# Expert 1's first weight matrix in 1 MB loads, one load of its second matrix at an earlier place, and VectorE's work beside the late tile in another order

## The chip, the cores and the metric

The kernel runs on one core of a Trainium2 chip. The metric is the device time of one execution in microseconds (us); times shown are medians of several executions on one chip. Beside these times there is one execution taken by the hardware profiler, from which every row below comes.

## The reference

Attention with decay gives a token matrix x of 3072 rows (4 batches of 768) by 512 (8 heads of 64). Each row then goes through one of 16 experts, which two small products choose.

```python
for t in range(S):                                   # S = 768, per batch and head
    state = gamma * state + outer(k[t], v[t])        # 64 x 64
    y[t] = scale * q[t] @ state
x = y.transpose(0, 2, 1, 3).reshape(3072, 512)
g = argmax(x @ w_group)                              # 4 groups
e = argmax(x @ w_expert[g])                          # 4 experts in a group
weight = softmax(group logits)[g] * softmax(expert logits)[e]
out[row] = weight * (relu(x[row] @ w1[g, e]) @ w2[g, e])   # 512 -> 1024 -> 512
```

## The kernel before, in words

**Two parts.** Attention runs in 12 steps of 128 tokens of two batches at once; what a step gives is written to `xd`, the matrix x in DRAM (the writes are those of line L356, on SyncE's queue). The router works on blocks of 4 chunks of 128 tokens while attention still runs: for every token it finds the expert, its rank in that expert's list (the rank matmuls L436 and L438), and adds the token to the lists by matmuls with one-hot matrices (`tally`, L522).

**Expert tiles.** An expert's tokens are gathered from `xd` by an indirect DMA on GpSimd (L775), transposed on TensorE (`tpx`, L793), split into a bf16 high part `xbh` (ScalarE, L795) and a low part `xbl` (VectorE, L818), and multiplied with the weights. The weights are loaded in f32 (`wf`, four buffers of 1 MB: two halves of w1, two of w2) and split likewise into `wh` (ScalarE, L751) and `wl` (VectorE, L753), eight pieces for one expert. Each product is three matmuls: high by high, high by low, low by high. The first layer goes to `hps` (L841, four quarters `f2`), and its relu is split into `hh` (ScalarE, L845) and `hl` (VectorE, L848).

**Order of the tiles.** Expert 0 comes in two: `ua`, its first 128 tokens, starts before attention has ended, and `ub`, the late tile (108 wide), takes the rest. Then follows `va` (expert 1, 236 wide), and then the other 14 experts, sorted on the chip by their number of tokens. The sort is `order()` on VectorE: `cnt`, `key`, two memsets, `gt` (L607), `pos` (L612), `eq` (L615), `eqk` (L620), `ordf` (L623), `ord` (L626). `own_counts()` then gives `ocols` (L583, L585), the width of `va`'s two parts, and `counts()` gives `cols` (L639 to L645), the widths of the sorted experts.

**How a width reaches TensorE.** `shape()` loads a width from memory into a register of TensorE's own sequencer (L806) and sets a shape from it (MOVE_SHAPE, L807). TensorE's sequencer works in program order, so matmuls behind such a load wait with it. The two loads of `ocols` stand behind the second and third part of `ub`'s second layer (L947), and the two loads of `cols` for the next expert in `va`'s first layer.

**What sets the order.** Nothing here is scheduled by a tool: the order on every engine is the order of the calls. `self.layers(u)` is a generator that stops between parts of a tile's matmuls, and the loops around it put other work at a stop numbered `i`. `first(n)` lets `ua`'s matmuls run n stops on; a stop in the first layer is 12 matmuls. `route_steps(n)` runs n steps of the router or of the sort. `beside(i, place)` puts loads and splits at places of attention step i.

Of the kernel before, what the change touches and what calls it, by code (L numbers as in the profile page):

```python
# [99 lines left out]


KX = (4, 6)
NEXT = {(10, 0): (0, 4), (10, 2): (4, 8)}
KEYED = (9, 10)


class Kernel:
# [1098 lines left out]
    def run(self):  # L1206
        tc, nc = self.tc, self.nc
        with ExitStack() as ctx:
# [18 lines left out]
            us = [dict(at=((j + 1) % 2, 0), W=(PW[-1:] + WIDTH)[j], pool=wpool[(j + 1) % 2]) for j in range(NS + 1)]  # L1227
            va = us[0]
# [4 lines left out]
            def pick(j):  # L1233
                self.picked(us[j], j - 1)

            def cols(j, i):
                return self.cols[0:1, i, j - 1:j] if j else self.own[:, i:i + 1]

            def first(n):

                for _ in range(n):
                    next(self.first, None)

            def early(i, k, high):
                if 0 <= i - 3 < 8:
                    self.wsplit(ua, 2 * i - 6 + k, 16, nc.gpsimd, high=high, low=not high)
# [9 lines left out]
            def beside(i, place):  # L1256

                last = i == NS2 - 1
                for k in range(*NEXT.get((i, place), (0,))):
                    self.wload_part(va, k)  # L1260
                if place == 5 and i == 10:
                    ua["mt"] = self.pairs()
                    self.tokens(ua["mt"][:, 0, 0:1], ua["mt"][:, 0, 1:2], self.lists[:, 0:1])
                    self.gather(ua)
                    self.known()
                if place == 0:
                    if 2 <= i <= 9:
                        for k in range(2):
                            self.wload_part(ua, 2 * i - 4 + k)
                if place == 4 and last:  # L1270
                    self.shape(ua, 4, 0, self.early_cols)
                if place == 0 and last:
                    early(i - 1, 0, False)
                    early(i - 1, 1, False)
                if place == 2 and last:
                    self.wsplit(va, 0, low=False)
                if place == 1:
                    if not last:
                        early(i - 1, 0, False)
                if place == 3 and last:  # L1280
                    self.xtrans(ua, "big", (0,))
                    self.wload(va, 2, nc.scalar)

            self.wp = pool("wp", 2)
            with ExitStack() as actx:
                apool = lambda name, bufs: actx.enter_context(tc.tile_pool(name=name, bufs=bufs))
                self.lp, self.vp = apool("lp", 1), apool("vp", 1)
                self.attention(extra, beside)
# [19 lines left out]
            late.append(self.late_entries(5, self.oh[:, 0:BM, 0:1]))  # L1308
            self.route_steps(99, True)
            assert not self.steps  # L1310
            first(3)
            self.wsplit(va, 2, low=False)
            next(route)
            while next(route) != "late":
# [8 lines left out]
                nc.vector.scalar_tensor_tensor(*h)  # L1323
            for _ in route:
                pass
            first(2)
            p, y = self.at
            ent = self.entries(5, *self.chosen(y, self.yp))
            self.spreads.append((self.marks(p, self.yp), ent))
# [2 lines left out]
            nc.gpsimd.memset(self.xg[1], 0.0)  # L1332
            self.wsplit(va, 3, low=False)
            self.steps.append(self.order())
            self.route_steps(5)
            for i, k in enumerate(self.first):
                if i == 0:
                    self.wsplit(va, 4, low=False)
# [5 lines left out]
                if i == 3:  # L1344
# [3 lines left out]
                    self.nc.vector.tensor_copy(ub["mt"][:, 0, 1:2], self.final[:, 0, 1, 1:2])  # L1348
                    va["mt"] = self.final[:, 1]
                    self.gather(va)  # L1350
            self.route_steps(99)
            assert not self.steps
            pick(1)
            pick(2)
            for u in us[1:3]:
                self.listed(u)
            self.own_counts()
            self.wsplit(va, 0, high=False)
            ub["wh"], ub["wl"] = ua["wh"], ua["wl"]
            self.gather(us[1])  # L1360
            for i, k in enumerate(self.layers(ub)):
                if i in (1, 3):
                    self.wsplit(va, 6 + i // 2, low=False)
                if i in (8, 12):
                    self.xtrans(va, ("sta", "big")[i // 4 - 2], (i // 4 - 2,))
                if i in (3, 7, 12, 13, 14):
                    low = (3, 7, 12, 13, 14).index(i) + 1
                    self.wsplit(va, low, high=False)
                    if low % 2:
                        self.wload(us[1], low // 2)  # L1370
                if i in (9, 10):
                    self.shape(va, 0, i - 9, cols(0, i - 9))
                if i == 15:
                    self.counts()
# [83 lines left out]
```

## Time and profile before

| | us |
|---|---|
| median of 3 runs | 406.8 (406.68 to 407.85) |
| the profiled execution | 405.67 |
| its span, first to last instruction | 403.9 |
| TensorE busy | 389.8 (97% of the span) |
| VectorE busy | 295.3 (73%) |
| ScalarE busy | 223.0 (55%) |
| GpSimd busy | 166.8 (41%) |

The profiled execution lasts 1.77 us longer than its span, and lies 1.13 us under the median of the runs. A busy share is a mean over the whole span; the stage that the change touches lies between 88 and 135 us, around the end of attention (about 104 us), and is read by itself. PE is TensorE's matmuls and PEld its weight loads, DVE is VectorE, ACT ScalarE, POOL GpSimd, SP SyncE; a q behind a name is the engine's sequencer.

### The profile page before, as it was taken

The page shows a single profiled execution, that of the slowest core. Times are in us where ns is not written, and L with a number is a line of the kernel's source. Part 1 is how long each engine was busy: PE and PEld are TensorE (multiplying, and loading weights), DVE is VectorE, ACT ScalarE, POOL GpSimd, SP SyncE. Part 2 cuts the span into 40 slices and gives each one's busy share as a digit, 9 for nine tenths or more (in the row PEclk, how much of TensorE's full clock was granted, in tenths as well). Part 3 has the DMA queues.
Part 4 walks back from the last instruction along what each step waited for, and adds up shares of the span by engine and source line. Part 5 has one row for each costly group of instructions (what it writes and reads, how often), then busy time and mean ns, then how long its engine had stood idle before and what let it go on. Part 6 is the DMA issues. An engine that isn't in the chain of part 4 may idle for free.

```text
span 403.9 us, 13857 instructions
## 1 busy us (share of the span) xinstructions
PE 389.8 (97%) x5809; PEld 324.4 (80%) x5841; DVE 295.3 (73%) x483; ACT 223.0 (55%) x340; POOL 166.8 (41%) x172
## 2 busy tenths in 40 slices
PE   9999999999998999999999999999999999999992
PEld 5789888888858878586978888797887978879792
DVE  4575876868798879886758686776878769788620
ACT  3224434544652765565566666676666767667520
POOL 4542769659585106131416234260522505232001
PEclk9999999999999999999999999999999999999997
DMA  7999999988816897887868787979789897887001
GB/s 254 356 346 346 317 355 292 355 283 290 288 69 208 304 363 263 264 262 246 252 228 267 258 298 262 299 276 320 260 282 330 274 325 268 256 333 278 11 32 36
DMA packets 38643, 107.13 MB, mean 265 GB/s; under 512 B 12020, under 2 KB 12148, under 8 KB 31156
## 3 DMA queue, kind: packets, MB, share of 16 engines
q1 hardware_dynamic: 28752, 92.52, 67.0%
q0 software_dynamic: 9536, 12.63, 8.9%
q10 hardware_dynamic: 292, 1.08, 0.8%
q8 instruction: 47, 0.77, 0.7%
q14 instruction: 16, 0.13, 0.1%
HBM read 94.18 MB, written 13.20 MB: 266 GB/s over the span
## 4 chain that ended last, share of the span: by engine, by line
PE 46%; issue 36%; POOL 10%; DVE 4%; ACT 1%; DMA 1%; POOLq 0%; SPq 0%; ACTq 0%; DVEq 0%
PE hps L841 12%; POOL out L999 6%; PE op L299 5%; PE yps L875 5%; PE sh L235 5%; POOL xg L775 4%; PE op L286 3%; PE yps L922 3%; PE sh L345 2%; PE stp L261 2%; PE yps L925 2%; PE sh L319 1%; PE sh L220 1%; PE log L332 1%; PE tpx L793 1%
## 5 line engine op out<-in xcount | busy, mean ns | idle before, releaser
L753 DVE TENSOR_TENSOR wl<-wf,wh 128x1024 bf16<-128x1024 f32 x120 | 145.1, 1220 | 36.9 <-ACT wh L751 33.0
L751 ACT ACTIVATE wh<-wf 128x1024 f16<-128x1024 f32 (+1 forms) x136 | 133.6, 1001 | 0.1
L841 PE MATMUL hps<-xbl,wh 128*128 128x128 f16 (+16 forms) x544 | 128.4, 249 | 0.7 <-issue 0.5
L841 PE MATMUL hps<-xbh,wh 128*128 128x0 bf16 x544 | 125.9, 241 | 0.3 <-issue 0.3
L841 PE MATMUL hps<-xbh,wl 128*128 128x0 bf16 x544 | 125.9, 241 | 0.2 <-issue 0.2
L999 POOL DMA_INDIRECT out<-yo,mt x30 | 39.1, 1303 | 159.0 <-ACT yo L981 121.1
L841 PEld LDWEIGHTS <-wh 128*128 128x128 f16 x1088 | 94.9, 98 | 1.5 <-issue 0.9
L925 PEld LDWEIGHTS <-wh 128*128 128x128 f16 x768 | 47.1, 97 | 22.9
L845 ACT ACTIVATE hh<-hps 128x256 bf16<-128x256 f32 (+16 forms) x68 | 34.1, 503 | 43.6 <-PE hps L841 41.6
L775 POOL DMA_INDIRECT xg<-xd,mt x30 | 51.8, 1727 | 13.1 <-issue 5.2
L841 PEld LDWEIGHTS <-wl 128*128 128x128 bf16 x544 | 53.1, 98 | 1.6 <-issue 0.9
L247 DVE TENSOR_TENSOR pf<-sh,tri 128x512 f32<-128x512 f32 x48 | 30.6, 685 | 22.7 <-PE op L299 8.3
L795 ACT ACTIVATE xbh<-tpx 128x512 bf16<-128x512 f32 (+14 forms) x32 | 16.7, 523 | 45.9 <-PE tpx L793 45.9
L848 DVE SCALAR_TENSOR_TENSOR hl<-hps,hh 128x216 f16<-128x216 f32 (+15 forms) x64 | 36.6, 574 | 4.2 <-ACT hh L845 3.7
L922 PE MATMUL yps<-wh,hh 128*128 128x512 f16 x96 | 36.4, 379 | 0.0
L922 PE MATMUL yps<-wh,hl 128*128 128x512 f16 x96 | 36.4, 379 | 0.0
L922 PE MATMUL yps<-wl,hh 128*128 128x512 bf16 x96 | 36.3, 378 | 0.0
L818 DVE TENSOR_TENSOR xbl<-tpx,xbh 128x512 f16<-128x512 f32 (+14 forms) x32 | 19.1, 597 | 20.0 <-ACT xbh L795 20.0
L925 PEld LDWEIGHTS <-wl 128*128 128x128 bf16 x384 | 24.2, 97 | 11.4
L192 POOL TENSOR_TENSOR vs<-lv,cst 128x512 f32<-128x512 f32 x24 | 24.6, 1043 | 14.9 <-DMA lv<-qkv 9.9
L925 PE MATMUL yps<-hl,wh 128*128 128x108 f16 (+11 forms) x384 | 29.1, 198 | 0.0
L925 PE MATMUL yps<-hh,wh 128*128 128x0 bf16 x384 | 26.6, 190 | 0.0
(194 smaller groups left out, 599.1 us busy)
## 6 DMA issues: line engine op xcount, KB each, us to landing
wf<-w2p SPq DMA_DIRECT2D x29, 1024.0 KB
wf<-w1p SPq DMA_DIRECT2D x28, 1024.0 KB
lq<-qkv SPq DMA_DIRECT2D x24, 256.0 KB
lk<-qkv SPq DMA_DIRECT2D x24, 256.0 KB
lv<-qkv SPq DMA_DIRECT2D x24, 256.0 KB
xd<-xr SPq DMA_DIRECT2D x22, 256.0 KB
wf<-w1p SPq DMA_DIRECT2D x16, 256.0 KB
wf<-w2p SPq DMA_DIRECT2D x8, 256.0 KB
```

Of the source, the lines that this page charges most:

```text
L192: self.nc.gpsimd.tensor_tensor(o, v, g, ALU.mult)
L235: nc.tensor.matmul(self.sh[2 * u + par][64 * half:64 * half + 64, cs], kT[rs, ks:ks + 64], qT[rs, cs], start=True, stop=True, skip_group_c ...
L247: nc.vector.tensor_tensor(o, sc, tri, ALU.mult)
L751: nc.scalar.activation(u["wh"][i][:, cs], u["wf"][i][:, cs], AF.Copy)
L753: (eng or nc.vector).tensor_tensor(u["wl"][i][:, cs], u["wf"][i][:, cs], u["wh"][i][:, cs], ALU.subtract)
L775: nc.gpsimd.indirect_dma_start(out=xg[0:r, i, :], out_offset=None, in_=self.xd[0:n, :], in_offset=bass.IndirectOffsetOnAxis(ap=mt[0:r, i, ...
L841: nc.tensor.matmul(o, l[:, k, fs], m, start=(n == 0), stop=(n == 11), skip_group_check=True)
L845: nc.scalar.activation(hh[:, f, 0:W], hv[:, :, 0:W], AF.Relu)
L848: nc.vector.scalar_tensor_tensor(*rest)
L922: nc.tensor.matmul(big, h[:, k, 0:P], w[k], start=(n == 0), stop=(n == 23))
L925: nc.tensor.matmul(o, w[k][:, d * P:d * P + P], m, start=(n == 0 and d == 0), stop=(n == 23), skip_group_check=True,)
L999: s = nc.gpsimd.indirect_dma_start(out=self.out, out_offset=bass.IndirectOffsetOnAxis(ap=mt[0:r, i, 0:1].bitcast(U32), axis=0), in_=yo[0:r ...
```

## The change

- Expert 1's w1 is loaded by two DMAs of 1 MB (L725) where eight of 256 KB (L739) stood, at the same places of step 10, on SyncE's queue.
- The first half of its w2, which ScalarE's queue issues, moves from place 3 to place 2 of the last step.
- `ua`'s first layer runs four stops ahead of the last rank matmuls where three stood (48 matmuls for 36), and one stop less later, so that seven of its eight stops lie ahead of the late tile's ids (L563) where six did.
- `order()` is cut at other places: `gt` and `pos` come behind the late tile's `xbl` and the final lists, and `eq` to `ocols` come inside `ub`'s first layer. One `wl` piece that stood ahead of `ub`'s `hl` is put between them, and the others move back by one place.
- The gather of the third tile stands behind a later stop in the code; on GpSimd itself the order of instructions stays as it was.

```diff
-NEXT = {(10, 0): (0, 4), (10, 2): (4, 8)}
+NEXT = {(10, 0): 0, (10, 2): 1}
...
-                for k in range(*NEXT.get((i, place), (0,))):
-                    self.wload_part(va, k)
+                if (i, place) in NEXT:
+                    self.wload(va, NEXT[i, place])
...
                 if place == 2 and last:
                     self.wsplit(va, 0, low=False)
+                    self.wload(va, 2, nc.scalar)
...
                 if place == 3 and last:
                     self.xtrans(ua, "big", (0,))
-                    self.wload(va, 2, nc.scalar)
...
-            first(3)
+            first(4)
             self.wsplit(va, 2, low=False)
...
-            first(2)
+            first(1)
...
             self.steps.append(self.order())
-            self.route_steps(5)
+            self.route_steps(3)
...
-            self.route_steps(99)
-            assert not self.steps
-            pick(1)
-            pick(2)
-            for u in us[1:3]:
-                self.listed(u)
-            self.own_counts()
-            self.wsplit(va, 0, high=False)
+            self.route_steps(2)
             ub["wh"], ub["wl"] = ua["wh"], ua["wl"]
-            self.gather(us[1])
             for i, k in enumerate(self.layers(ub)):
...
-                if i in (3, 7, 12, 13, 14):
-                    low = (3, 7, 12, 13, 14).index(i) + 1
+                if i == 1:
+                    self.wsplit(va, 0, high=False)
+                if i == 3:
+                    self.route_steps(2)
+                if i == 7:
+                    self.route_steps(99)
+                    assert not self.steps
+                    pick(1)
+                    pick(2)
+                    for u in us[1:3]:
+                        self.listed(u)
+                    self.own_counts()
+                if i == 10:
+                    self.gather(us[1])
+                if i in (7, 12, 13, 14, 15):
+                    low = (7, 12, 13, 14, 15).index(i) + 1
                     self.wsplit(va, low, high=False)
```

On VectorE, just ahead of the late tile's `xbl`, the sort's first steps stand so (a minus marks a row of before alone, a plus one of after; `key` is the sort key):

```order
 L603 MEMSET key 128x1
 L604 MEMSET key 128x1
-L607 TENSOR_TENSOR gt<-key 128x256
-L612 TENSOR_REDUCE pos<-gt 128x16
 L818 TENSOR_TENSOR xbl<-tpx,xbh 128x4x108
 L529 TENSOR_TENSOR lists<-lists,tally 128x160
```

`gt` and `pos` no longer stand ahead of `xbl`. They come back on VectorE behind the last of the list's instructions (L535, L1348):

```order
 L535 TENSOR_REDUCE final<-lists 128x32
 L1348 COPY mt<-final 128x1
+L607 TENSOR_TENSOR gt<-key 128x256
+L612 TENSOR_REDUCE pos<-gt 128x16
+L848 SCALAR_TENSOR_TENSOR hl<-hps,hh 128x2x108
+L753 TENSOR_TENSOR wl<-wf,wh 128x1024
+L848 SCALAR_TENSOR_TENSOR hl<-hps,hh 128x2x108
 L615 TENSOR_TENSOR eq<-pos,rest 128x256
 L620 TENSOR_TENSOR eqk<-eq,rest 128x256
+L848 SCALAR_TENSOR_TENSOR hl<-hps,hh 128x2x108 x2
 L623 TENSOR_REDUCE ordf<-eqk 128x16
 L626 CAST ord<-ordf 128x16
```

Between L1348's copy and `ordf`, and so ahead of `ocols`, stand seven more instructions than before: `gt`, `pos`, four `hl` of the late tile and one `wl` piece of expert 1. On ScalarE, in the last attention step, the load of w2 stands so:

```order
 L391 ACTIVATE ex<-log 128x80
 L751 ACTIVATE wh<-wf 128x1024
+L725 DMA wf<-w2p 128x2048
 L324 ACTIVATE ls<-sh_117 128x256
 L353 ACTIVATE pf<-sh_118 128x512
 L353 ACTIVATE pf<-sh_119 128x512
 L795 ACTIVATE xbh<-tpx 128x4x128
-L725 DMA wf<-w2p 128x2048
 L324 ACTIVATE ls<-lgt 128x256
```

The load moved ahead of four instructions, among them the transposed output's copies `pf`, which the next writes to `xd` read.

## Rows read from the trace of the kernel before

**Rows 1.** Length, then busy us of PE, PEld, DVE, ACT, POOL; clock, DMA share, GB/s.

```profile
135.00:398.00 263.00, 261.31 (x3257) 214.86 (x3281) 198.08 (x234) 164.45 (x228) 82.80 (x54) 1.00 0.75 256
```

**Rows 2.** Timeline of PE: start, duration, line, tile, and the idle time before.

```profile
106.49 0.22 PE L841 MATMUL hps<-xbh,wl 128*128 128x0 bf16 x1
107.05 0.20 PE L436 MATMUL log<-oh,stri 128*128 128x80 bf16 x1 [0.34 <-ACT ex L409]
...
115.05 0.59 PE L793 MATMUL tpx<-ident,xg 108*128 108x108 f32 x4 [0.21 <-DVE hl L1330]
...
116.77 0.72 PE L522 MATMUL tally<-yT,hot 128*128 128x160 bf16 x8
...
117.59 0.20 PE L841 MATMUL hps<-xbh,wl 128*128 128x0 bf16 x1
118.00 0.40 PE L841 MATMUL hps<-xbl,wh 128*128 128x108 f16 x5 [0.21 <-DVE xbl L818]
...
120.17 0.21 PE L841 MATMUL hps<-xbl,wh 128*128 128x108 f16 x1
...
121.39 0.21 PE L841 MATMUL hps<-xbl,wh 128*128 128x108 f16 x1 [0.50 <-issue]
...
125.10 0.31 PE L947 MATMUL yps<-hh,wh 128*128 128x0 bf16 x4 [0.23 <-issue]
...
131.86 0.65 PE L994 MATMUL tpy<-ident,yT 128*108 128x128 f32 x4 [1.16 <-ACT yT L953]
...
134.52 0.26 PE L841 MATMUL hps<-xbl,wh 128*128 128x236 f16 x1
```

**Rows 3.** Timeline of DVE.

```profile
112.02 2.04 DVE L494 TENSOR_TENSOR yT<-rest,tile 128x128 bf16<-128x128 f32 x1
...
115.45 1.53 DVE L607 TENSOR_TENSOR gt<-key 128x256 f32<-128x256 f32 x1
...
117.86 0.31 DVE L529 TENSOR_TENSOR lists<-lists,tally 128x160 f32<-128x160 f32 x1
...
118.69 0.42 DVE L615 TENSOR_TENSOR eq<-pos,rest 128x256 f32<-128x256 f32 x1
...
119.61 0.42 DVE L623 TENSOR_REDUCE ordf<-eqk 128x16 f32<-128x256 f32 x1
...
120.53 0.20 DVE L585 TENSOR_SCALAR ocols<-ofc 1x1 int32<-1x1 f32 x2
...
121.79 0.65 DVE L848 SCALAR_TENSOR_TENSOR hl<-hps,hh 128x216 f16<-128x216 f32 x2
...
127.23 0.61 DVE L818 TENSOR_TENSOR xbl<-tpx,xbh 128x432 f16<-128x432 f32 x1 [1.34 <-ACT xbh L795]
127.76 3.48 DVE L753 TENSOR_TENSOR wl<-wf,wh 128x1024 bf16<-128x1024 f32 x3
...
132.07 0.17 DVE L644 SCALAR_TENSOR_TENSOR cols<-num,rest 128x14 int32<-128x14 f32 x1
```

**Rows 4.** The line that loads a width, 119 to 135: count, ns, first and last start.

```profile
L806 PEldq TENSOR_LOAD <-ocols x2: 302/306/311, 123.2 to 124.2; - x2
```

**Rows 5.** Timeline of POOL.

```profile
111.42 1.16 POOL L775 DMA_INDIRECT xg<-xd,mt  x1 [1.12 <-DVE eg L416]
...
115.43 1.27 POOL L501 TENSOR_TENSOR yT<-yT,pc 128x640 bf16<-128x640 bf16 x1
```

**Rows 6.** The gather line's waits on POOL's sequencer, 105 to 116: ns min/median/max.

```profile
L775 POOLq EVENT_SEMAPHORE  x4: 17/43/228, 110.1 to 110.4; - x4
```

**Rows 7.** Timeline of ACT.

```profile
98.45 1.05 ACT L751 ACTIVATE wh<-wf 128x1024 f16<-128x1024 f32 x1
...
102.88 0.36 ACTq L725 DMA_DIRECT2D wf<-w2p  x1
...
121.56 0.35 ACT L845 ACTIVATE hh<-hps 128x216 bf16<-128x216 f32 x1 [1.03 <-remote]
```

**Rows 8.** The same columns as Rows 1, two microseconds of attention's end.

```profile
100.00:102.00 2.00, 2.00 (x28) 1.47 (x24) 1.75 (x6) 0.90 (x3) 2.00 (x3) 1.00 0.19 75
```

## The prediction

> **What bounds the kernel now.** I read the table by stretches first. From 135 us to 398 us TensorE is busy for 261.31 of 263 us [rows 1], and the list of its waits has no entry there. So whatever moves the moment at which expert 1's tile gets through its first layer moves the end by as much, and nothing after it can give the time back. I take as the mark the third quarter (f2 = 2) of that layer, which starts at 134.52 [rows 2]: the first point behind the last hole.
>
> Then TensorE's timeline ahead of this mark, for its holes. The reader is to see six places. One is the rank matmul's: the matmul before it starts at 106.49, it itself at 107.05, with ScalarE's `ex` named. The late tile's transposes (115.05) wait a little. The first matmuls with `xbl` start at 118.00 behind VectorE's `xbl`, while the one before them, which needs none, started at 117.59. From 120.17 to 121.39 only two matmuls stand between the two that the rows show: 1.22 where these matmuls follow each other every 0.04 elsewhere in this quarter, so 1.1 is lost. That hole is put down to "issue", as is 0.23 at 125.10. The last is the wait of 1.16 for `yT` ahead of 131.86 [rows 2].
>
> Third, VectorE's and GpSimd's timelines, for what these holes hang on. `gt` takes 1.53 from 115.45 to 116.98, `eq`, of the same size, 0.42 [rows 3]. GpSimd's product L501 ends at 115.43 + 1.27 = 116.70 [rows 5], 0.28 before `gt` does. So `gt` stood behind L501, and `xbl` behind `gt`.
>
> **The change part by part.** The sum is made against the profiled execution, 405.67, which is 1.13 under the median of the runs; the difference is then laid on the median, 406.8.
>
> *Two loads for eight.* The bytes are the same. The first reader of w1, ScalarE's split at 98.45, has no wait on its row [rows 7], and nothing is queued behind SyncE's issues that is waited for there. I take 0. The bounds are 0 and a loss of what the split would wait; what it makes is used no sooner than expert 1's `xbl`, which ends at 127.84 [rows 3], so a late split costs only what ScalarE's next instruction waits.
>
> *w2 sooner.* The load goes out when the split has ended, 98.45 + 1.05 = 99.50, instead of 102.88, 3.38 earlier [rows 7]. It falls into a gap: from 100 to 102 the DMA engines are busy for 0.19 and move 75 GB/s [rows 8], against 256 as a mean later [rows 1]. At 256 GB/s a load of 1.05 MB takes 4.1 us (an estimate from that row), so most of it is gone before the last writes to `xd`, and these land earlier. The late tile's gather waits for them: GpSimd is free 1.12 before it starts at 111.42 [rows 5], at 110.30. But its sequencer's longest wait there is 0.23 [rows 6]. So the gather gains between 0.1 and 1.12: the low end if the rest of the 1.12 is its own cost.
>
> The Trainium skill ("DMA: Bandwidth & Descriptors", Issuing engines are not separate DMA queues) says that DMAs of different issuing engines run on the same 16 engines and interleave. That speaks against a gain from the place alone: by it the load takes from other transfers as much as it leaves to `xd`. Row 100 to 102 shows the engines mostly idle there, which is why I count some gain; by the rule alone the gather would keep its time and the sum below would be that of the fourth case.
>
> *Ranks behind 48 matmuls.* Twelve matmuls move ahead of the rank matmul and fill its hole: 107.05 - 106.49 = 0.56 from start to start, 0.34 of it idle by the row [rows 2]; I take 0.5. The ranks themselves come at most 0.1 later. With the 0.21 of idle time ahead of the transposes at 115.05, and about as much again if one counts from start to start, TensorE can bring the tally forward by at most 0.9. It needs GpSimd's second L501 too, which follows the gather. I call g the gain at the tally: between 0.1 and 0.9, and take 0.5.
>
> *gt and pos behind the lists.* `xbl` no longer stands behind `gt`, so the hole at 118.00 goes: 118.00 - 117.59 = 0.4 [rows 2]. What `gt` costs at its new place, behind L501's end, I take from `eq`: 0.42 for 1.53. L494 (2.04 at 112.02) is the other VectorE row that ran so long beside an L501 [rows 3]. Were 1.53 `gt`'s own time, `ocols` would come 1.1 later and the sum below be +1.9.
>
> The Trainium skill ("SBUF — State Buffer", Who interferes with whom) has a rule for this: a VectorE instruction with two inputs in SBUF and a GpSimd instruction that reads SBUF exclude each other for a whole instruction. L494 and `gt` agree; by this rule the new `gt`, beside indirect DMAs, isn't held up.
>
> *The widths come later.* This is the price. TensorE's sequencer wants `ocols` at 123.2 [rows 4], or 1.1 earlier without the issue hole. Before, `ocols` were there at 120.53 + 0.20 = 120.73 [rows 3]. Now VectorE begins the lists at 117.49 - g + 0.06 = 117.55 - g, and then follow:
> - lists, ids, weights, copy: 118.69 - 117.86 = 0.83
> - `gt`, `pos`, by `eq` and `eqk`: 0.9
> - `hl`: 0.33 (half of 0.65), `wl`: 3.48 / 3 = 1.16, `hl`: 0.33
> - `eq`, `eqk`: 119.61 - 118.69 = 0.92
> - two more `hl`: 0.65
> - `ordf` to the second `ocols`: 120.73 - 119.61 = 1.12
>
> Together 6.24 [rows 3], so `ocols` are there at 123.8 - g, three microseconds later than before and behind the sequencer, which reaches the load at 121.7 - g (123.2 less the 1.1 less the 0.4). The matmuls of `ub`'s second layer queued behind that load wait. And one more term: the second of these `hl` needs ScalarE's `hh` of 121.56, which came late because of TensorE's issue hole, or of its signal (1.03, "remote") [rows 7]. VectorE reaches that `hl` at 117.55 + 0.83 + 0.90 + 0.33 + 1.16 = 120.77 - g; `hh` ended at 121.56 + 0.35 = 121.91, now 0.4 + g earlier, 121.5 - g. If the lag recurs, VectorE waits 0.7 and `ocols` come at 124.5 - g.
>
> From the first load (123.2) to the first matmul behind the second (125.10) it is 1.9 [rows 2, 4]. So that matmul starts at 126.4 - g with the lag and at 125.7 - g without it, against 125.10: +1.3 - g or +0.6 - g.
>
> *From there to the mark.* Before, 134.52 - 125.10 = 9.42. After, TensorE's own path is the same 9.42 if the wait for `yT` comes back. The other path goes through VectorE: `xbl` of expert 1's second part ends at 127.84, 2.74 behind the 125.10; then now four `wl` for three, and the counts: 132.07 + 0.17 - 127.84 = 4.40, plus 1.16, is 5.56; then a load of `cols`, half of 1.9. That is 9.25. So even if the wait for `yT` (1.16) disappears, the mark can't come more than 0.17 sooner: what the order of the `wl` pieces gave to `ub` is asked back at the counts. The third tile's weights and token lists also come later by some microseconds; their first use lies behind the mark, so I cost them at 0.
>
> **Sum.** With the lag and g = 0.5: 1.3 - 0.5 = +0.8. The profiled execution would go from 405.67 to 406.5, the median from 406.8 to 407.6.
>
> **The rivals.**
> 1. *The lag at `hh` recurs* (my forecast, +0.8; with g from 0.9 to 0.1 it is +0.4 to +1.2, 407.2 to 408.0). For it: the hole comes while the gathers of expert 1 run, and these stand as before behind the lists. Against it: the profile names no cause.
> 2. *No lag:* +0.6 - g = +0.1, 406.9 (406.6 to 407.3). The early start of the late tile and the late widths then pay for each other.
> 3. *The issue holes belong to the profiled execution alone,* before and after. Then before the matmul of 125.10 would start 1.1 + 0.2 earlier, at 123.8, and after at 125.7 - g: 1.9 - g = +1.4, 408.2 (407.8 to 408.6). Against it: the runs are no faster than the profiled execution.
> 4. *w2's load moves nothing,* g = 0.1, with the lag: +1.2, 408.0.
> 5. *Faster:* the widths come in time after all. Place: the load L806. It decides where `ocols` are there before the sequencer is, so the chain of 6.24 would have to be some 2 us shorter, for which I see only `hl` and `wl` pieces that cost less than their rows. Then the start of the late tile stays won, g + 0.4 = 0.9, and if the wait for `yT` goes too, 1.2 more: 405.9 to 404.7.
>
> **How the numbers follow.** About 0.3%, 1.2 us, is what a measurement of this kernel can tell from no change. Chances: first case 0.42, second 0.24, third 0.12, fourth 0.08, fifth 0.14. Slower by over 0.3% is above 408.0: two thirds of the third, most of the fourth, and four tenths of the first, which ends there and whose terms aren't good to 0.2; together 0.32. Faster is below 405.6, three quarters of the span from 405.9 to 404.7: 0.11. The rest is 0.57. The range leaves out the faster half of the fifth and what lies beyond the third's far end: 405.4 to 408.8. The likeliest time is the first case's, 407.6.
>
> **What would show it.** No hole ahead of the rank matmul; the gather of the late tile at 110.5 to 111.3; `gt` at 0.42; `xbl` of the late tile right after `xbh` and no wait at its first matmuls. `ocols` at 123.3 to 124.1, and TensorE's sequencer waiting there, so that a hole of 1 to 3 us stands in L947; whether `hh` of the second quarter has a lag; the third quarter of expert 1's first layer at 134.9 to 135.7. I am wrong if `ocols` are in time, if g is far above 0.9, or if the mark moves and the end doesn't follow it.

## The result, and the profile after

The change made the kernel slower: 408.69 us median of 22 executions against 406.81 of 22 before, ratio 1.0068 with a 95% interval of 1.0048 to 1.0089, about 2.8 us. The medians differ by 1.88; ratios, here and below, are of fast executions alone. The profiled execution took 408.28 against 405.67, its span 406.5 against 403.9. The forecast was 407.6, or +0.8: the right side, under a third of the size.

The mark of the prediction, the third quarter of expert 1's first layer, moved from 134.52 [rows 2] to 136.87, and the span grew by 2.6. Here is TensorE's timeline of the changed kernel, with the columns of [rows 2]:

```profile
102.28 0.66 PE L793 MATMUL tpx<-ident,xg 128*128 128x128 f32 x4 [0.57 <-DMA xg<-xd,mt]
...
107.36 0.20 PE L436 MATMUL log<-oh,stri 128*128 128x80 bf16 x1
...
115.48 0.59 PE L793 MATMUL tpx<-ident,xg 108*128 108x108 f32 x4 [1.11 <-DVE hl L1330]
...
117.21 0.73 PE L522 MATMUL tally<-yT,hot 128*128 128x160 bf16 x8
...
118.08 0.40 PE L841 MATMUL hps<-xbl,wh 128*128 128x108 f16 x5
...
121.25 0.20 PE L841 MATMUL hps<-xbh,wh 128*128 128x0 bf16 x1 [0.34 <-issue]
...
121.98 0.20 PE L841 MATMUL hps<-xbh,wl 128*128 128x0 bf16 x1 [0.40 <-issue]
...
122.71 0.21 PE L841 MATMUL hps<-xbh,wl 128*128 128x0 bf16 x1 [0.32 <-issue]
...
123.50 0.36 PE L947 MATMUL yps<-hl,wh 128*128 128x108 f16 x4
...
126.69 0.31 PE L947 MATMUL yps<-hh,wh 128*128 128x0 bf16 x4 [1.56 <-DVE ocols L585]
...
127.65 0.31 PE L947 MATMUL yps<-hh,wh 128*128 128x0 bf16 x4 [0.30 <-issue]
...
132.69 0.60 PE L994 MATMUL tpy<-ident,yT 128*108 128x128 f32 x4
...
136.87 0.26 PE L841 MATMUL hps<-xbl,wh 128*128 128x236 f16 x1 [1.39 <-DVE hl L848]
```

The hole ahead of the ranks is gone (107.36 has no wait), and so are the one at `xbl` (118.08) and the wait for `yT` (132.69). New are a wait of 0.57 for expert 0's own gather ahead of its first transposes, 1.11 ahead of the late tile's, 1.56 for `ocols`, and 1.39 ahead of the mark, where the sequencer waits for the counts (`cols`, ready at 136.16); the profile names the `hl` that follows them on VectorE.

Two rows of the kernel before that were not shown yet, the start of expert 0's transposes and of the late tile's second layer, let one cut the stage into pieces:

```profile
102.15 0.63 PE L793 MATMUL tpx<-ident,xg 128*128 128x128 f32 x4
...
122.75 0.35 PE L947 MATMUL yps<-hl,wh 128*128 128x108 f16 x4
```

GpSimd's gather of that tile and its landing, of the kernel before:

```profile
97.15 1.28 POOL L775 DMA_INDIRECT xg<-xd,mt  x1 [0.32 <-DVE pre L541]
```

```profile
DMA to landing us min/median/max: 4.4/4.4/4.4
```

GpSimd of the changed kernel:

```profile
96.55 1.28 POOL L775 DMA_INDIRECT xg<-xd,mt  x1 [0.32 <-DVE pre L541]
...
111.33 1.16 POOL L775 DMA_INDIRECT xg<-xd,mt  x1 [0.88 <-DVE sms L413]
112.52 1.28 POOL L501 TENSOR_TENSOR yT<-yT,pc 128x640 bf16<-128x640 bf16 x1
114.40 0.79 POOL L429 TENSOR_SCALAR pc<-wt 128x4 bf16<-128x4 f32 x1 [0.60 <-DVE wt L426]
...
116.18 1.26 POOL L501 TENSOR_TENSOR yT<-yT,pc 128x640 bf16<-128x640 bf16 x1
```

The execution after was 0.60 ahead at that gather (96.55 against 97.15). It was already 0.58 ahead as the first load of w1 was issued (88.58 against 89.16), the first thing that the change touches. From the gather on:

| piece | before | after | difference |
|---|---|---|---|
| gather's issue to expert 0's transposes | 5.00 | 5.73 | +0.73 |
| to the tally | 14.62 | 14.93 | +0.31 |
| to the late tile's second layer | 5.98 | 6.29 | +0.31 |
| to the matmul behind both `ocols` loads | 2.35 | 4.15 | +1.80 |
| to the mark | 9.42 | 9.22 | -0.20 |

Together +2.95; less the 0.60 it is the mark's +2.35. The first piece is w2. ScalarE's timeline after shows why:

```profile
97.84 0.36 ACTq L725 DMA_DIRECT2D wf<-w2p  x1
97.86 1.05 ACT L751 ACTIVATE wh<-wf 128x1024 f16<-128x1024 f32 x1
...
122.74 0.35 ACT L845 ACTIVATE hh<-hps 128x216 bf16<-128x216 f32 x1 [2.36 <-PE hps L841]
```

The load stands behind the split in ScalarE's order, but it is issued as the split begins, at 97.84. That is 1.3 after the gather's start, while the gather is in flight. In the six other runs in which ScalarE issues it here, it too goes out within 0.04 of the split's start. DMA shares, with the columns of [rows 1], show the former gap filled:

```profile
98.00:100.00 2.00, 2.00 (x38) 1.54 (x35) 1.86 (x7) 0.91 (x1) 2.00 (x2) 1.00 0.84 179
100.00:102.00 2.00, 1.72 (x21) 1.51 (x17) 1.16 (x5) 1.47 (x3) 2.00 (x3) 1.00 0.96 395
...
140.00:398.00 258.00, 258.00 (x3218) 211.77 (x3242) 195.36 (x230) 161.64 (x224) 81.55 (x53) 1.00 0.76 261
```

From 100 to 102 the share is 0.96 where it was 0.19 [rows 8], and TensorE is busy for 1.72 of 2.00. From 140 on TensorE never stops, so what is lost ahead stays lost. VectorE after:

```profile
111.66 2.18 DVE L421 TENSOR_SCALAR u<-sms 128x4 f32<-128x4 f32 x1
...
117.97 0.32 DVE L529 TENSOR_TENSOR lists<-lists,tally 128x160 f32<-128x160 f32 x1 [0.70 <-PE tally L522]
...
118.81 0.42 DVE L607 TENSOR_TENSOR gt<-key 128x256 f32<-128x256 f32 x1
...
123.13 0.38 DVE L848 SCALAR_TENSOR_TENSOR hl<-hps,hh 128x216 f16<-128x216 f32 x1 [1.98 <-ACT hh L845]
...
125.61 0.20 DVE L585 TENSOR_SCALAR ocols<-ofc 1x1 int32<-1x1 f32 x2
...
129.79 0.61 DVE L818 TENSOR_TENSOR xbl<-tpx,xbh 128x432 f16<-128x432 f32 x1 [2.25 <-ACT xbh L795]
130.31 4.62 DVE L753 TENSOR_TENSOR wl<-wf,wh 128x1024 bf16<-128x1024 f32 x4
...
135.75 0.17 DVE L644 SCALAR_TENSOR_TENSOR cols<-num,rest 128x14 int32<-128x14 f32 x1
```

`gt` costs 0.42 at its new place, and `ocols` come at 125.81, 1.98 of it a wait for `hh` (ScalarE's 122.74), behind the three issue holes.

### The profile page after: what moved, and what is told of

Read it like the earlier page. It is cut to its first block, busy times and chain, and to the rows that moved or that the text cites. A ratio compares the mean times of both kernels' runs of the same rounds, so it can differ in the third digit from the quotient of the medians.

```text
span 406.5 us, 13842 instructions
## 1 busy us (share of the span) xinstructions
PE 390.4 (96%) x5809; PEld 324.9 (80%) x5841; DVE 293.8 (72%) x483; ACT 222.9 (55%) x340; POOL 166.4 (41%) x172
## 4 chain that ended last, share of the span: by engine, by line
PE 43%; issue 36%; POOL 10%; DVE 7%; DMA 1%; ACT 1%; POOLq 0%; DVEq 0%; ACTq 0%
PE hps L841 11%; POOL out L999 6%; PE yps L875 5%; PE op L299 4%; PE sh L235 4%; POOL xg L775 4%; PE yps L922 3%; PE sh L345 2%; PE op L286 2%; PE stp L261 2%; PE yps L925 2%; DVE wl L753 1%; DMA xg<-xd,mt 1%; PE sh L220 1%; DVE pf L247 1%
```

## The experiments

Sixteen runs, each timed in five rounds beside the kernel before on the same chip. Ratios are to the kernel before, with 95% intervals.

| run | parts that it has | ratio | interval |
|---|---|---|---|
| the change | loads, w2, ranks, order | 1.0068 | 1.0048 to 1.0089 |
| w2_only | w2 | 1.0094 | 1.0058 to 1.0129 |
| order_only | order | 1.0005 | 0.9979 to 1.0031 |
| ranks_only | ranks | 0.9997 | 0.9970 to 1.0025 |
| loads_only | loads | 0.9973 | 0.9944 to 1.0003 |
| loads_w2 | loads, w2 | 1.0015 | 0.9979 to 1.0050 |
| loads_ranks | loads, ranks | 1.0005 | 0.9981 to 1.0029 |
| loads_order | loads, order | 1.0021 | 1.0001 to 1.0041 |
| w2_back | loads, ranks, order | 1.0035 | 1.0000 to 1.0070 |
| no_order | loads, w2, ranks | 1.0056 | 1.0019 to 1.0092 |
| w2_sp | w2, on SyncE's queue | 1.0065 | 1.0032 to 1.0098 |
| w2_nogather | w2, without expert 0's gather | 0.9983 | 0.9956 to 1.0010 |
| w2_parts | w2 in four loads | 1.0023 | 0.9992 to 1.0053 |
| w2_half | half of w2 | 1.0022 | 0.9991 to 1.0052 |
| best1 | ranks, another order | 0.9991 | 0.9960 to 1.0021 |
| best2 | best1 and loads | 0.9980 | 0.9956 to 1.0003 |
| best3 | loads, gt, scatter later | 1.0004 | 0.9980 to 1.0029 |

**The parts one by one, and one taken back.**

w2_only, on the kernel before:
```diff
                 if place == 2 and last:
                     self.wsplit(va, 0, low=False)
+                    self.wload(va, 2, nc.scalar)
...
                     self.xtrans(ua, "big", (0,))
-                    self.wload(va, 2, nc.scalar)
```


> The kernel before with w2's load sooner and nothing else. In the changed kernel expert 0's first transposes waited 0.6 for their own gather, which ran beside this load. Theory 1 (the load takes DMA time from that gather): the same wait here, expert 0's first tile 0.7 later against attention, some of it caught by later waits; 406.8 to 407.6, ratio 1.000 to 1.002. Theory 2 (the load falls into a gap, as forecast): no wait, the late tile's gather up to 1 sooner, ratio 0.998. Theory 3 (the load alone makes the loss): ratio 1.006.

order_only has the changed kernel's `route_steps` and stops `i`, with the loads, w2 and `first()` of before; on the changed kernel that is:
```diff
-NEXT = {(10, 0): 0, (10, 2): 1}
+NEXT = {(10, 0): (0, 4), (10, 2): (4, 8)}
...
-                    self.wload(va, 2, nc.scalar)
...
                     self.xtrans(ua, "big", (0,))
+                    self.wload(va, 2, nc.scalar)
...
-            first(4)
+            first(3)
...
-            first(1)
+            first(2)
```

> The kernel before with VectorE's new order alone (gt and pos behind the lists, eq to ocols inside the late tile's first layer). Theory 1 (the late widths make most of the loss): TensorE waits 1 to 2 for ocols, expert 1's third quarter 1.3 to 2.0 later, ratio 1.003 to 1.005. Theory 2 (the other parts make the loss): no more than +0.3, ratio 1.000 to 1.001.

ranks_only:
```diff
-            first(3)
+            first(4)
             self.wsplit(va, 2, low=False)
...
-            first(2)
+            first(1)
```


> The kernel before with 48 matmuls ahead of the ranks and nothing else. Theory 1 (the late tile's start hangs on GpSimd and on VectorE's last hl of expert 0's first tile, not on TensorE): the hole of 0.5 ahead of the ranks goes and comes back ahead of the late tile's transposes, ratio 1.000. Theory 2 (the filled hole is won): the tally 0.5 sooner, ratio 0.9988.

w2_back is the changed kernel with the diff of w2_only turned round.

> The changed kernel with w2's load back at its old place. Theory 1 (the load costs by itself beside the late widths): expert 0's transposes don't wait for their gather, 0.7 of the 2.8 comes back, ratio to before 1.005. Theory 2 (the late widths alone): ratio unchanged, 1.007. Theory 3 (the load makes the loss): 1.000.

w2 alone costs 0.94%, more than the whole change. Its first transposes, on TensorE:

```profile
104.66 1.12 PE L793 MATMUL tpx<-ident,xg 128*128 128x128 f32 x4 [3.36 <-DMA xg<-xd,mt]
```

and the landing of their gather, which is issued at 96.14 here:

```profile
DMA to landing us min/median/max: 8.5/8.5/8.5
```

The gather takes 8.5 where it took 4.4, and TensorE stands for 3.36. So theory 1 has the mechanism, and the size is above even theory 3's: the wait is six times the 0.57 of the changed kernel, from which I had taken it.

The loss is more than this wait. TensorE's granted clock behind it, in stretches of 2 us with the columns of [rows 1]:

```profile
104.00:106.00 2.00, 1.34 (x8) 0.92 (x12) 0.00 (x0) 0.18 (x1) 0.00 (x0) 0.56 0.34 130
106.00:108.00 2.00, 2.00 (x14) 1.28 (x7) 1.49 (x3) 0.87 (x3) 0.58 (x1) 0.50 0.11 37
108.00:110.00 2.00, 2.00 (x16) 2.00 (x15) 0.53 (x3) 1.79 (x3) 0.00 (x0) 0.50 0.32 125
```

The clock stood at 1.00 (2.4 GHz) up to the wait, and at 0.50 (1.2 GHz) from its end to about 111, while TensorE was busy again. The first transposes take 1.12 for 0.63. From them to the late tile's transposes it is 15.27 us (104.66 to 119.93); in the six profiled executions with an early load and no fall of the clock it is 13.0 to 13.2. So the clock costs some 2 us here, an estimate from these rows. The times fit: the mean granted clock is 0.991 or less in 8 of the 9 executions of w2_only, and in 10 of 134 of the kernel before.

The ranks alone give nothing, as theory 1 says. Its profiled execution, the slowest of its 13, has another wait there, though: 2.69 for the late tile's gather. The order alone is as theory 2 has it, with an interval that reaches theory 1; w2_back lies between theories 1 and 3.

**With the large loads.** loads_only on the kernel before; loads_w2 adds the diff of w2_only:
```diff
-NEXT = {(10, 0): (0, 4), (10, 2): (4, 8)}
+NEXT = {(10, 0): 0, (10, 2): 1}
...
-                for k in range(*NEXT.get((i, place), (0,))):
-                    self.wload_part(va, k)
+                if (i, place) in NEXT:
+                    self.wload(va, NEXT[i, place])
```

> The kernel before with w1 in two 1 MB loads and nothing else. Theory 1 (the larger loads are done sooner and free the DMA engines ahead of expert 0's gather): DMA share between 96 and 98 under 0.8 where it was 1.00, the gather lands no later than 4.4 after its issue, ratio 0.998 to 1.000. Theory 2 (they cost by themselves): 1.002 or more.

> The kernel before with the 1 MB loads and w2's load sooner. The run with the early w2 alone had expert 0's gather land 8.5 after its issue (4.4 before) and lost 0.94%. Theory 1 (what is left of w1's small loads and the early w2 together crowd the gather; with 1 MB loads w1 is out of the way): it lands about 5.5 after its issue, ratio 1.002 to 1.004. Theory 2 (the early w2 costs the same with either kind of load): 1.009.

loads_only is as its theory 1 has it, though its interval reaches 1: the DMA share from 96 to 98 is 0.66 and the gather lands 4.2 after its issue. With the large loads the early w2 costs less: 1.0015 / 0.9973 = 1.0042. TensorE's first transposes in loads_w2:

```profile
102.85 0.66 PE L793 MATMUL tpx<-ident,xg 128*128 128x128 f32 x4 [0.90 <-DMA xg<-xd,mt]
```

They wait 0.90, not 3.36. DMA shares in w2_only and then in loads_w2, just before the gather starts and as it runs:

```profile
96.00:98.00 2.00, 2.00 (x37) 1.76 (x36) 0.87 (x4) 1.77 (x5) 1.82 (x2) 1.00 1.01 383
```

```profile
96.00:98.00 2.00, 2.00 (x40) 1.60 (x41) 1.04 (x6) 1.76 (x5) 1.68 (x2) 1.00 0.50 185
```

With small loads the DMA engines are still full when w2 comes; with large ones they are half free. So the two parts belong together, and the large loads hid about half of what the early w2 costs.

**Which way w2 acts.** w2_sp issues the early load from SyncE; w2_nogather is w2_only without the gather of expert 0's first tile; w2_parts splits the early load into four of 512 columns; w2_half puts columns 0 to 1023 at the early place and the rest at the old one.

```diff
-                    self.wload(va, 2, nc.scalar)
+                    self.wload(va, 2)
```


> The kernel before with w2's load at the early place, but issued by SyncE's queue, behind the writes to xd there and what is left of w1. Theory 1 (a further queue takes turns with the gather's queue and so slows it): expert 0's gather lands within 6 of its issue, its transposes wait under 1, ratio 1.000 to 1.003. Theory 2 (the bytes count, whatever queue carries them): it lands 8 or more after its issue, ratio 1.009.

```diff
-                    self.gather(ua)
+                    ua["xg"] = self.xg[0]
```


> The kernel before with the early w2 alone, and without the gather of expert 0's first tile, whose tokens stay zeros (it leaves that gather out). Theory 1 (all that the early w2 costs passes through this gather): no wait at the first transposes, and the 0.94% of the early w2 is gone, ratio 1.000 or under. Theory 2 (it also costs through the later writes to xd or in the late tile): 1.004 or more.

```diff
-                    self.wload(va, 2, nc.scalar)
+                    wf = va["wf"][2] = self.wst.tile([P, 2048], F32, name="wf", tag="wf", bufs=4)
+                    for h in range(4):
+                        nc.scalar.dma_start(wf[:, h * 512:h * 512 + 512], self.a_w2[1, 0][:, h * 512:h * 512 + 512])
```


> The kernel before with the early w2 as four loads of 256 KB, whose rows are 2 KB like the gather's, where the one load has rows of 8 KB. Theory 1 (queues take turns packet by packet, so large packets crowd out the gather's small ones): the gather lands within 6.5 of its issue (8.5 with the one load), ratio 1.002 to 1.005. Theory 2 (the bytes of the load and of w1's tail share one limit, whatever their packets): 8 or more, ratio 1.009.

```diff
-                    self.wload(va, 2, nc.scalar)
+                    wf = va["wf"][2] = self.wst.tile([P, 2048], F32, name="wf", tag="wf", bufs=4)
+                    nc.scalar.dma_start(wf[:, 0:1024], self.a_w2[1, 0][:, 0:1024])
...
                     self.xtrans(ua, "big", (0,))
+                    nc.scalar.dma_start(va["wf"][2][:, 1024:2048], self.a_w2[1, 0][:, 1024:2048])
```


> The kernel before with half of this w2 load (512 KB) at the early place and half at the old one. Theory 1 (the delay goes with the bytes that are early): the gather lands about 6.5 after its issue, the transposes wait about 1.3, ratio 1.003 to 1.005. Theory 2 (the issue alone, or the first packets, make the delay): 8 or more, 1.009.

Without the gather the early w2 costs nothing, 0.9983, and none of the 12 executions has a mean clock of 0.991 or less. That speaks for theory 1: the loss passes through this one gather. The kernel before without the gather was not run, and the tile's tokens are zeros here, so it is not a difference of one thing alone. Landing of the gather in w2_parts, then in w2_half:

```profile
DMA to landing us min/median/max: 5.8/5.8/5.8
```

```profile
DMA to landing us min/median/max: 5.9/5.9/5.9
```

The same megabyte in rows of 2 KB delays the gather by 1.4 over the 4.4 of before, in rows of 8 KB by 4.1; half of it with rows of 4 KB by 1.5. Without an early load the landings lie between 3.8 and 5.2, one profiled execution each. What the load's queue moved from 97.5 to 101.5 (packets, MB, share of the DMA engines' time), in w2_only and then in w2_parts:

```profile
q10 hardware_dynamic: 56, 0.46, 32.8%
```

```profile
q10 hardware_dynamic: 240, 0.45, 34.7%
```

The bytes are the same there, the packets four times as many. So the bytes are not all, and the size of the load's rows counts. The Trainium skill ("DMA: Bandwidth & Descriptors", Queues, rings and completion order) says that a DMA engine takes turns between queues packet by packet; these three landings agree with it. It is not the rows alone either: in the changed kernel the same queue moved 0.57 MB in 70 packets in that stretch, and TensorE waited only 0.57. Moving the load to SyncE's queue doesn't help by the times (1.0065, nearer to theory 2). Its trace agrees: the gather lands 8.2 after its issue, TensorE waits 3.11, the clock falls to 0.50 behind that, and 9 of its 12 executions have a mean clock of 0.991 or less.

**The order, with nothing else late.** no_order is the changed kernel with VectorE's order of before, loads_order is order_only with the large loads, loads_ranks is ranks_only with them.

> The changed kernel with VectorE's order of before (large loads, early w2 and the ranks stay). Theory 1 (the late widths cost about 2 in the changed kernel, and w2 the rest): ratio to before 1.001 to 1.002, no wait for ocols or for the counts. Theory 2 (the early w2 alone makes the loss, and the order is free as it is in the kernel before): 1.006 to 1.007.

> The kernel before with the large loads and VectorE's new order. The large loads alone gave 0.9973, the order alone 1.0005. Theory 1 (the order costs wherever nothing else is late): 1.001 to 1.003, with a wait of more than 1 for ocols, or for hl behind the counts. Theory 2 (the order is free): 0.998.

> The kernel before with the large loads and 48 matmuls ahead of the ranks. Theory 1 (the ranks' hole is given back ahead of the late tile's transposes): as the large loads alone, 0.997. Theory 2 (the ranks' new place costs, by VectorE's work sliding into GpSimd's): 1.000 or more, with a VectorE row of 2 beside the late tile's gather.

no_order is nearer to its theory 2 and loads_order as its theory 1 has it, so the two disagree on what the order costs; loads_ranks is as its theory 2 in time, with the VectorE row of 2 that the kernel before has too. Four pairs differ by the order alone: order_only to the kernel before, +0.05%; loads_order to loads_only, +0.48%; w2_back to loads_ranks, +0.30%; the change to no_order, +0.12%. Their mean is 0.24%, 1.0 us; in no pair do the two intervals lie apart, so that the order costs anything is not shown by itself, and the size is rough. Three pairs with the large loads differ by w2 alone: +0.42%, +0.51% (no_order to loads_ranks) and +0.33% (the change to w2_back), mean 0.42%, 1.7 us. Here too the intervals overlap in each pair. Some of it may be the clock again: with the early w2 and the large loads 13 of 43 executions have a mean clock of 0.991 or less, in the partners without it 5 of 36. TensorE's waits from 104 to 140 in w2_back, then in loads_ranks:

```profile
PE tpx L793 <- DMA xg<-xd,final: 1.5, 1, 1.5
PE hps L841 <- DVE hl L848: 1.4, 1, 1.4
PE tpx L793 <- DVE hl L1330: 0.9, 1, 0.9
```

```profile
PE tpx L793 <- DMA xg<-xd,final: 1.3, 1, 1.3
PE tpx L793 <- DVE hl L1330: 0.9, 1, 0.9
PE yps L947 <- DVE hl L848: 0.4, 1, 0.4
```

Neither has issue holes in `hps`. TensorE then runs ahead and waits for expert 1's gather (1.5 and 1.3); no wait for `ocols` is listed, so I read that wait as its cover. What differs is the 1.4 ahead of the mark, behind the counts. And the 0.9 for `hl` in both is the filled hole of the ranks, given back.

**Towards a faster version.** best1 has `first(4)`, `route_steps(3)` with `eq` to `ocols` straight behind the lists, VectorE's weight steps ahead of three `hl` and the fourth `hl` ahead of L494, and expert 0's scatter behind expert 1's gathers. best2 adds the large loads; best3 has the large loads, `route_steps(3)` and the later scatter alone. The core of best1:
```diff
-            for h in self.held[:3]:
-                nc.vector.scalar_tensor_tensor(*h)
             for _ in route:
                 pass
-            first(2)
+            for h in self.held[:3]:
+                nc.vector.scalar_tensor_tensor(*h)
+            first(1)
+            nc.vector.scalar_tensor_tensor(*self.held[3])
...
-            nc.vector.scalar_tensor_tensor(*self.held[3])
...
-            self.route_steps(5)
+            self.route_steps(3)
+            self.later = []
...
                     self.gather(va)
+                    later, self.later = self.later, None
+                    for s in later:
+                        self.scatter(*s)
```

> The kernel before with what the runs speak for, and w2's load at its old place: 48 matmuls ahead of the ranks; gt and pos behind the lists, but eq to ocols straight behind them; VectorE's weight steps ahead of three hl and the fourth hl ahead of L494; expert 0's scatter behind expert 1's two gathers on GpSimd. Theory 1 (expert 1's gather and the late tile's transposes set the mark): both 0.5 to 0.8 sooner, ratio 0.998. Theory 2 (GpSimd's chain from the late tile's gather to the second L501 sets it): no gain, 1.000.

> The kernel of the run best1 with the large loads. If the gains add, best1's 0.9991 and the loads' 0.9973 give 0.9964; if the large loads only move a wait that best1's other orders bring back, 0.999.

> The kernel before with the large loads, gt and pos behind the lists with eq to ocols straight behind them, and expert 0's scatter behind expert 1's gathers on GpSimd; ranks, w2 and VectorE's other work as before. Theory 1 (the large loads give 0.2%, and expert 1's gather comes up to 0.8 sooner): 0.996. Theory 2 (the gather isn't what the mark waits for): as the large loads alone, 0.997 to 0.999.

The gains don't add, and best3 is slower than either of its theories. loads_only and best2 are under 1 by 0.2 to 0.3%, and both intervals reach 1, so no version is shown to beat the kernel before.

## Why the prediction was right or wrong

**What bounds it: right.** The mark moved by 2.35 and the span by 2.6.

**w2 sooner: wrong, and the step that failed.** The prediction said that the load goes out at 99.50, when the split has ended, and "falls into a gap", so that the late tile's gather comes sooner. It went out at 97.84, as the split began (97.86): in these traces the DMA behind the split didn't wait for the split to end. Expert 0's gather was in flight, which I hadn't put on the list of what the load could meet. At the old place the load stood behind `xbh`, whose transposes wait for that very gather, so its place kept the two apart. w2_only shows the cost, and w2_nogather, with the reserve named there, that it passes through this gather. It is 0.94% with the small loads, where a fall of the clock behind the wait adds to it, and some 0.42%, 1.7 us, with the large ones. The late tile's gather gained 0.09 (111.33 for 111.42), less than the 0.60 that this execution was ahead. The sentence that I let weigh against the gain, that DMAs of all issuing engines share the same 16 engines, held, and I priced it as "no gain" only.

**Ranks: the hole went, its worth didn't come.** I put it into g = 0.5. The transposes of the late tile wait for VectorE's `hl` instead, 1.11 in the changed kernel and 0.9 in w2_back; the runs give 0.9997 alone. So g was about 0 from this part.

**VectorE's weights slid into GpSimd's work.** `u` (L421) took 2.18 from 111.66, as long as L494 did before; behind it `wt` came late, GpSimd waited 0.60 for it, and the second L501 began at 116.18 for 115.43 [rows 5]. The tally came 0.44 later (117.21 for 116.77), not 0.5 sooner. The prediction has no term for this, and it comes with the early w2, not with the ranks. In w2_only, which has VectorE's order of before, `u` is held too; in w2_back, which has the ranks and the new order, it is L494:

```profile
116.28 2.00 DVE L421 TENSOR_SCALAR u<-sms 128x4 f32<-128x4 f32 x1
```

```profile
112.02 2.17 DVE L494 TENSOR_TENSOR yT<-rest,tile 128x128 bf16<-128x128 f32 x1
```

All seven profiled executions with the early w2 and expert 0's gather hold `u` or the row behind it (L423), and their second L501 begins 4.8 to 5.2 after the late tile's gather; in the eleven others it is 3.6 to 4.2. What this alone costs at the mark was not tried.

**gt, xbl: right.** 0.42, and no hole at 118.08.

**The widths: the chain was right, the size of one wait not.** Lists to `ocols` took 125.81 - 117.97 = 7.84, of which 1.98 is the wait for `hh`; without it 5.86, where I summed 6.24. I gave that wait 0.7. The two loads took 127.65 - 125.81 = 1.84 for 1.9, and the rest to the mark 9.22 for 9.25, with the wait for `yT` gone and the counts in its place, as the prediction has it. Without the issue holes the prediction's second case gave +0.6 - g; with g at 0 that is +0.6, and the runs' mean for the order is 1.0.

**The lag recurs: in the profile, not as a rule.** The holes in `hps` put down to issue stand in the profiled executions of the kernel before, of the change, loads_only, loads_w2, best1 and w2_sp, and not in those of the other twelve. No edit is common to the six that have them. None of the six waits for expert 1's gather ahead of its transposes; of the twelve others all but best3 do, by 0.8 to 1.9. So the holes and that wait may cover for each other; that is argued, and the cause of the holes stays open.

So of 2.8 us about 1.7 are w2 and 1.0 the order by the pairs; what the ranks and loads do besides is within the intervals. The pieces of the one profiled execution divide it otherwise, 1.0 up to the tally, 0.3 to the late tile's second layer and 1.6 from there to the mark, so the shares are rough. The prediction had the second and the wrong sign for the first.

## What to carry to other kernels

Before a load is moved forward, list the transfers in flight at the new place, and ask who waits for the smallest of them: a small gather on the path pays for a large load beside it. An order in which the load stands behind a reader of that gather may be what protects it. And look up when a DMA is issued in the trace, by the start of the instruction ahead of it, not by its end. Where TensorE waits, read the granted clock behind the wait too: the 3.36 of w2_only cost some 2 us more that way.

## What the runs showed of the hardware that was not expected

Beside w1's small loads the early 1 MB load put 4.1 us on a gather of 128 rows of 2 KB; four loads of the same bytes put 1.4 on it.

VectorE's stall of about 2 beside GpSimd's gather and product isn't tied to one instruction. In each of the 18 profiled executions one VectorE instruction that began 0.3 to 0.9 into the late tile's gather instruction took 1.6 to 2.7, and ended 0.03 to 0.56 behind the end of the product after it. It was L494 in the kernel before (2.04 from 112.02, where the product began only at 112.61), and elsewhere `u`, L423, `hot`, `cnt` or `gt`. `u` of four columns (2.18) has one input; it began 0.86 before the product and ended 0.04 behind its end at 113.80. Unheld, `u` takes 0.22 (in the kernel before) and would have ended ahead of the product, so the hold can begin while the gather's instruction still runs. What the prediction says of two inputs does not cover this.
